# Seven products of quarters for u times w1 in a linear attention and feed-forward kernel

## The chip, the cores and the metric

The kernel runs on one core of a Trainium2 chip. The time is the device time of one execution in microseconds (us), as the median of several runs; the profile is one execution of its own, with a time of its own.

## What is computed

There are 8 batches of 576 rows and 8 heads of 64 columns, so 512 columns in all. The reference, cut to what matters:

```python
kv  = einsum('bhsd,bhse->bhde', k, v)            # per batch and head
out = einsum('bhsd,bhde->bhse', q, kv)
x   = out / sqrt(mean(out * out, -1) + 1e-6) * g_norm
x   = x.transpose(0, 2, 1, 3).reshape(8, 576, 512)
h   = x.transpose(0, 2, 1) @ U @ V               # mixes the rows, rank 32
u   = x + h.transpose(0, 2, 1)
y   = u + maximum(u @ w_ch1, 0) @ w_ch2          # 512 -> 2048 -> 512
```

## The kernel before

All data are float32. To keep the accuracy, the large products are made in three: each factor is split into a high part (rounded to float32r) and a low part (the rest), and high x high, high x low and low x high are added in PSUM.

The rows of u are handled transposed, as four tiles of 128 columns (index c or d) by rows. The 8 x 576 rows are cut into nine **blocks** of 512 (NBLK). Block j needs the end of batch j - 1 and the beginning of batch j. In each block a loop over 16 values of **f** (128 columns of the hidden layer each) makes h for f (`ffn1`, L429: 4 values of d x 3 matmuls of 512 columns, into the one bank of `ps_h`), takes relu and splits it (`relu`, L436: ACT writes the high part hh, DVE the low part hl), and adds the y of the f before (`ffn2`, L445: 4 outputs c x 3 matmuls of 512 columns, into the four banks of `ps_y`). Each matmul has a weight load of its own. In the last block the fourth output is made in two halves of 256 columns, and the last three f's are put together (L757). `finish` (L452) adds u to y, on DVE and POOL, and stores it, after f = 0 of the next block.

All weights stay in SBUF, decoded and split in block 0, in tiles `w_f` with the high and low parts of w1 and w2 for one f (for f = 0 and 1 in tiles of their own).

While block j runs, the kernel **prepares** batch j + 1, in steps placed between the f's by `prep_schedule` (L674) with the distances of `STEPS`. For each of the four pairs of heads p: `kv_step` (L247) makes k times v and loads the next pair; `out_step` (L276) makes q times kv in two PSUM banks; `stats_step`, `mul_step` and `xsplit_step` normalise and split; `turn_step` (L331) transposes in pieces of 32 on DVE and places them by 16 transfers on SP (L343) in `ut32[p]`; then `t_step`, `t4_step` and `mix_step` (L419) multiply by U and V and add (L426) into `ut32[p]`. `split_cols` (L376) writes the factors of the next block, high part on ACT and low part on DVE. The banks for these steps come from `ps_p`, which has three.

All loads and stores are issued by SP. Each engine works its instructions off in a fixed order that a planner of the tile framework sets when the program is built: an instruction earlier in the code goes first, but one that would have to wait can be passed by one that is ready. The start (`ORDER0`) is written out by hand and isn't touched by the change.

Of the kernel before, what the change touches and what calls it, by code (L numbers as in the profile page):

```python
# [10 lines left out]
F32 = mybir.dt.float32  # L11
F32R = mybir.dt.float32r
# [9 lines left out]
P = 128  # L22
# [29 lines left out]
LATE = 8  # L52
LATER = 0
NBLK = B * S // BLK
ABS_LO = float(np.array([897 << 20], np.uint32).view(np.float32)[0])
# [4 lines left out]
def build(ctx: ExitStack, tc: tile.TileContext, kv_in, kvt0_in, kvt_in, q_in, uv_in, g_in, w_in, out):  # L60
# [3 lines left out]
    ldp = ctx.enter_context(tc.tile_pool(name="ldp", bufs=1))  # L64
    utp = ctx.enter_context(tc.tile_pool(name="utp", bufs=2))
    hp = ctx.enter_context(tc.tile_pool(name="hp", bufs=2))
# [8 lines left out]
    x_sb = const.tile([P, NT, P], F32, name="x")  # L75
    ut32 = [const.tile([P, S], F32, name=f"ut32_{c}") for c in range(ND)]
    ident = const.tile([P, P], F32, name="ident")
# [155 lines left out]
    def ut_of(j):  # L233
        if j not in ut:
            ut[j] = [utp.tile([P, ND, BLK], F32R, name=f"ut{s}") for s in "hl"]
        return ut[j]
# [139 lines left out]
    def split_cols(b, c, part, lo_eng):  # L376

        m = BLK * (b + 1) - S * b
        uh, ul = ut_of(b + part)
        if part == 0:  # L380
            src, lo = ut32[c][:, 0:m], BLK - m
        else:
            src, lo = ut32[c][:, m:S], 0
        n = src.shape[-1]
        hi, lo = uh[:, c, lo:lo + n], ul[:, c, lo:lo + n]
        if b == 0:
            split(hi, lo, src, lo_eng)
        else:
            nc.scalar.mul(out=hi, in_=src, mul=g_sb)  # L389
            nc.vector.scalar_tensor_tensor(out=lo, in0=src, scalar=g_sb, in1=hi.bitcast(F32),  # L390
                                           op0=ALU.mult, op1=ALU.subtract)
# [6 lines left out]
    def mix_first(p):  # L398

        s = state[0, p]  # L400
        main = s["main"]
        for a in (0, 2):
            own = main.rearrange("p (i a j) -> p i a j", a=4, j=32)[:, :, a:a + 2]
            v = v4[:, QO[a]:QO[a] + 2 * QL[a]].rearrange("p (a t) -> p a t", a=2)[:, :, 0:P]
            nc.tensor.matmul(own, lhsT=s["t4"], rhs=v.rearrange("p a (i j) -> p i a j", j=32), start=False, stop=(a == 2))
        uh, ul = ut_of(0)
        move("uh", p, uh[:, p], main, g_sb)
        nc.vector.scalar_tensor_tensor(out=ul[:, p], in0=main, scalar=g_sb, in1=uh[:, p].bitcast(F32),
                                       op0=ALU.mult, op1=ALU.subtract)
# [9 lines left out]
    def mix_step(b, p):  # L419
        t4 = state.pop((b, p))["t4"]  # L420
        n = S // 2
        for lo in (0, n):
            mp = bank()[:, 0:n]
            nc.tensor.matmul(mp, lhsT=t4, rhs=v4[:, lo:lo + n], start=True, stop=True)  # L424
            own = ut32[p][:, lo:lo + n]
            nc.vector.tensor_tensor(out=own, in0=mp, in1=own, op=ALU.add)  # L426
        split_cols(b, p, 0, nc.vector)

    def ffn1(h, f, ds, j):  # L429
        uh, ul = ut[j]  # L430
        for d in ds:
            nc.tensor.matmul(h, lhsT=w1s[f][0][:, d, :], rhs=uh[:, d, :], start=(d == 0), stop=False)  # L432
            nc.tensor.matmul(h, lhsT=w1s[f][0][:, d, :], rhs=ul[:, d, :], start=False, stop=False)  # L433
            nc.tensor.matmul(h, lhsT=w1s[f][1][:, d, :], rhs=uh[:, d, :], start=False, stop=(d == ND - 1))  # L434

# [16 lines left out]
    def finish(y, j):  # L452
        uh, ul = ut.pop(j)
        for c, cols, acc in y:
            if j == NBLK - 1:
                o = ut32[c][:, S - BLK + cols.start:S - BLK + cols.stop]
                nc.vector.scalar_tensor_tensor(out=o, in0=o, scalar=g_sb, in1=acc, op0=ALU.mult, op1=ALU.add)
            else:
                o = st.tile([P, DM], F32, name="st")
                nc.vector.tensor_tensor(out=o, in0=acc, in1=uh[:, c, :].bitcast(F32), op=ALU.add)  # L460
                nc.gpsimd.tensor_tensor(out=o, in0=o, in1=ul[:, c, :].bitcast(F32), op=ALU.add)  # L461
            nc.sync.dma_start(out=out[j, c][:, cols], in_=o)

    def outputs(j):

        y = [(c, slice(0, BLK), ps_y.tile([P, BLK], F32, name="y")) for c in range(ND)]
        if j == NBLK - 1:
            c, _, acc = y.pop()
            y.append((c, slice(0, BLK // 2), acc[:, 0:BLK // 2]))
            y.append((c, slice(BLK // 2, BLK), ps_p.tile([P, BLK], F32, name="pp")[:, 0:BLK // 2]))  # L470
        return y

    top = const.tile([P, 2 * DM], U32, name="top")
# [107 lines left out]
    def first_pair(p):  # L581
# [10 lines left out]
        uh, ul = ut_of(0)  # L592
        uh, ul = uh[:, p], ul[:, p]
        xv = x.rearrange("p i (h e) -> p i h e", e=D)
# [79 lines left out]
    def prep_schedule(b):  # L674

        todo = {}
        if 0 < b <= B:
            if b == 1:
                for p in range(NPAIR):
                    todo[REST + 2 * p] = [lambda p=p: mix_rest(p), lambda p=p: split_cols(0, p, 1, nc.vector)]  # L680
            else:
                todo[1] = [lambda: [split_cols(b - 1, c, 1, nc.vector) for c in range(ND)]]
        if b < B:
            for p in range(NPAIR):
                steps = STEPS0 if b == 1 else STEPS
                base = steps["gap"] * p
# [32 lines left out]
    y_prev = hprev = None  # L719
    held = []  # L720
    for j in range(NBLK):
        todo = prep_schedule(j + 1)
        y = None
        for f in range(NF):
            if j == 0:
                while ahead < min(NF, f + 1 + AHEAD):
# [3 lines left out]
                    ahead += 1  # L730
            end = False
            if j == 0 and f == 1:
                ffn2(y, [hprev])
            if j == 0 and f == 0:
                h = h_bank
            else:
                end = j == NBLK - 1 and f == NF - 1
                h = ps_p.tile([P, BLK], F32, name="pp") if end else ps_h.tile([P, BLK], F32, name="h")
                ffn1(h, f, range(ND), j)
            hcur = (f, *relu(h, end))  # L740
            steps = todo.get(2 * f, [])
            for w in steps:
                in_block(j, f, w)
            if hprev is not None and not (j == NBLK - 1 and f > NF - 3) and not (j == 0 and f == 1):
                ffn2(y_prev if f == 0 else y, [hprev])
# [4 lines left out]
            for w in todo.get(2 * f + 1, []):  # L750
                in_block(j, f, w)
            if j == 0 and LATE + f - LATER < NF and f >= LATER:
                load_w(LATE + f - LATER)
            held = (held + [hcur])[-3:]
            hprev = hcur
        y_prev = y
    ffn2(y, held)  # L757
    finish(y, NBLK - 1)


# [54 lines left out]
```

## Time and profile before

| | |
|---|---|
| median of 3 runs | 925.65 us (925.32 to 926.26) |
| the profiled execution | 925.44 us, span 923.7 us |
| TensorE busy | 909.7 us, 4532 matmuls |
| VectorE / ScalarE / GpSimd busy | 402.4 / 271.3 / 47.8 us |
| read from and written to HBM | 46.97 MB and 9.44 MB |
| mean granted TensorE clock | 0.998 |

In the profile, PE is TensorE's matmul, PEld its weight load, DVE VectorE, ACT ScalarE, POOL GpSimd, SP the engine that issues transfers. A group row gives line, engine, operation, what is written and read, the shape and the count; then busy us, the mean ns of one, the idle time of the engine just before them, and what ended it. A row of the waits gives who waited for whom, the us in total, how often, and the longest. A row of the timeline gives start, duration, engine, line, operation and count. Matmuls overlap in the pipeline, so the pace is read from start to start and not from the duration of one.

### The profile page before, as it was taken

To read this page: it belongs to the slowest core of one execution; us is meant where nothing else is said; L and a number is where in the kernel's file an instruction comes from. 1 tells how busy PE (TensorE), PEld (TensorE's weight loads), DVE (VectorE), ACT (ScalarE), POOL (GpSimd) and SP (SyncE) were. 2 spreads that over 40 slices of the span, in tenths; PEclk is the share of its full clock that TensorE was granted. 3 is DMA by queue.
4 is the path that set the end of the run, shared out by engine and by line. 5 is a ranking of instruction groups with operands and counts; after the bars stand their busy time and mean duration, and the time that the engine had idled before them with its cause. 6 is when DMAs were issued, how large, how long until landed. Compare 5 with 4: busy or idle time off the path is not lost.

```text
span 923.7 us, 12114 instructions
## 1 busy us (share of the span) xinstructions
PE 909.7 (98%) x4532; PEld 759.3 (82%) x4532; DVE 402.4 (44%) x870; ACT 271.3 (29%) x572; POOL 47.8 (5%) x61
## 2 busy tenths in 40 slices
PE   8899999999999999999999999999999999999998
PEld 7678888888878888888888888888788888888887
DVE  5789974534344435434344445434334331112112
ACT  5677742322222223222222223222222121111110
POOL 2000002000110002000200010000200020002000
PEclk9999999999999999999999999999999999999999
DMA  9952223211121112212121111212111010001001
GB/s 344 418 202 72 88 68 100 86 32 58 49 81 56 42 62 94 59 32 77 51 60 55 55 65 58 81 32 71 58 49 27 14 46 1 0 1 46 1 1 46
DMA packets 43019, 65.48 MB, mean 71 GB/s; under 512 B 9680, under 2 KB 27856, under 8 KB 42960
## 3 DMA queue, kind: packets, MB, share of 16 engines
q1 hardware_dynamic: 42960, 64.70, 21.0%
q8 instruction: 36, 0.59, 0.3%
q14 instruction: 23, 0.19, 0.1%
HBM read 46.97 MB, written 9.44 MB: 61 GB/s over the span
## 4 chain that ended last, share of the span: by engine, by line
PE 69%; DVE 1%; DMA 0%; POOL 0%; issue 0%; DVEq 0%; POOLq 0%
PE y L449 31%; PE h L432 11%; PE h L433 11%; PE h L434 11%; PE pp L261 2%; PE pp L284 2%; DVE utl L390 1%; PE pp L449 1%; PE pp L354 1%; PE pp L424 0%; PE pp L356 0%; DMA out<-st 0%; DVE st L460 0%; PE pp L286 0%; DVE hl L442 0%; POOL st L461 0%
## 5 line engine op out<-in xcount | busy, mean ns | idle before, releaser
L449 PE MATMUL y<-hh,ws 128*128 128x512 f32 x1000 | 327.9, 394 | 0.0
L442 DVE SCALAR_TENSOR_TENSOR hl<-h,hh 128x512 fp32r<-128x512 f32 x143 | 98.6, 689 | 318.9 <-ACT hh L441 317.7
L449 PEld LDWEIGHTS y<-hh,ws 128*128 128x128 f32 x1000 | 180.9, 188 | 33.1 <-issue 0.2
L441 ACT ACTIVATE hh<-h 128x512 fp32r<-128x512 f32 x143 | 85.4, 597 | 405.4 <-PE h L434 405.4
L432 PE MATMUL h<-uth,ws 128*128 128x512 f32 x500 | 198.0, 396 | 2.1 <-DVE hl L442 2.1
L433 PE MATMUL h<-utl,ws 128*128 128x512 f32 x500 | 195.7, 391 | 0.0
L434 PE MATMUL h<-uth,ws 128*128 128x512 f32 x500 | 195.4, 391 | 0.0
L449 PE MATMUL y<-hl,ws 128*128 128x512 f32 x500 | 193.4, 387 | 0.0
L432 PEld LDWEIGHTS h<-uth,ws 128*128 128x128 f32 x500 | 94.2, 188 | 25.0 <-DVE hl L442 4.3
L434 PEld LDWEIGHTS h<-uth,ws 128*128 128x128 f32 x500 | 94.2, 188 | 20.4
L449 PEld LDWEIGHTS y<-hl,ws 128*128 128x128 f32 x500 | 93.9, 188 | 19.3
L433 PEld LDWEIGHTS h<-utl,ws 128*128 128x128 f32 x500 | 94.4, 189 | 18.5
L461 POOL TENSOR_TENSOR st<-st,utl 128x512 f32<-128x512 f32 x32 | 41.1, 1305 | 782.0 <-DVE st L460 780.6
L449 PE MATMUL y<-hh,w2s 128*128 128x512 f32 (+1 forms) x144 | 47.6, 395 | 2.6 <-ACT hh L441 2.6
L426 DVE TENSOR_TENSOR ut<-pp,ut 128x288 f32<-128x288 f32 x56 | 25.0, 455 | 46.0 <-DMA ut<-xt 30.5
L389 ACT ACTIVATE uth<-ut,g_sb 128x448 fp32r<-128x448 f32 (+7 forms) x56 | 27.6, 531 | 47.7 <-DVE ut L426 25.8
L460 DVE TENSOR_TENSOR st<-y,uth 128x512 f32<-128x512 f32 x32 | 21.4, 686 | 40.3 <-PE y L449 29.1
L449 PEld LDWEIGHTS y<-hh,w2s 128*128 128x128 f32 x144 | 26.5, 188 | 9.4 <-ACT hh L441 4.5
L390 DVE SCALAR_TENSOR_TENSOR utl<-ut,g_sb,uth 128x448 fp32r<-128x448 f32 (+7 forms) x56 | 26.9, 513 | 14.1 <-POOL st L461 6.9
L300 DVE TENSOR_REDUCE sums<-x 128x10 f32<-128x640 f32 x28 | 22.9, 818 | 20.6 <-ACT x L288 20.3
L261 PE MATMUL pp<-kv_sb 128*128 128x128 f32 x224 | 30.3, 274 | 0.0
L284 PE MATMUL pp<-kvb,q_sb 128*128 128x128 f32 x224 | 29.5, 274 | 0.0
(188 smaller groups left out, 852.4 us busy)
## 6 DMA issues: line engine op xcount, KB each, us to landing
kv_sb<-kv_in SPq DMA_DIRECT2D x29, 512.0 KB, 3.5
raw<-w_in SPq DMA_DIRECT2D x14, 1023.6 KB, 15.2
q_sb<-q_in SPq DMA_DIRECT2D x29, 288.0 KB, 2.8
out<-st SPq DMA_DIRECT2D x32, 256.0 KB, 2.0
ut<-xt SPq DMA_DIRECT2D x224, 20.0 KB, 1.8
ut<-xt SPq DMA_DIRECT2D x224, 16.0 KB, 1.8
kvt_sb<-kvt_in SPq DMA_DIRECT2D x27, 128.0 KB, 3.1
kvq<-kv_in SPq DMA_DIRECT2D x3, 512.0 KB, 7.3
```

The costliest lines, as they stand in the source:

```text
L261: nc.tensor.matmul(pp[:, 0:P], lhsT=m[:, i * P:(i + 1) * P], rhs=m[:, MAIN + i * P:MAIN + (i + 1) * P], start=(i == 0 and b < NATIVE), sto ...
L284: nc.tensor.matmul(big[:, i * P:(i + 1) * P], lhsT=qt[:, TAIL + i * P:TAIL + (i + 1) * P], rhs=kb, start=True, stop=True)
L389: nc.scalar.mul(out=hi, in_=src, mul=g_sb)
L390: nc.vector.scalar_tensor_tensor(out=lo, in0=src, scalar=g_sb, in1=hi.bitcast(F32), op0=ALU.mult, op1=ALU.subtract)
L426: nc.vector.tensor_tensor(out=own, in0=mp, in1=own, op=ALU.add)
L432: nc.tensor.matmul(h, lhsT=w1s[f][0][:, d, :], rhs=uh[:, d, :], start=(d == 0), stop=False)
L433: nc.tensor.matmul(h, lhsT=w1s[f][0][:, d, :], rhs=ul[:, d, :], start=False, stop=False)
L434: nc.tensor.matmul(h, lhsT=w1s[f][1][:, d, :], rhs=uh[:, d, :], start=False, stop=(d == ND - 1))
L441: last["relu"] = nc.scalar.activation(out=hh, in_=h, func=AF.Relu)
L442: nc.vector.scalar_tensor_tensor(out=hl, in0=h, scalar=0.0, in1=hh.bitcast(F32), op0=ALU.max, op1=ALU.subtract)
L449: nc.tensor.matmul(acc, lhsT=w2s[f][w][:, c, :], rhs=h[:, cols], start=(f == 0 and w == 0 and h is hh), stop=(f == NF - 1 and w == 1))
L461: nc.gpsimd.tensor_tensor(out=o, in0=o, in1=ul[:, c, :].bitcast(F32), op=ALU.add)
```

## The change

In blocks 0 and 1 the work is as before. From block 2 (FAST) on, u times w1 is made for two f's at a time, a **group** g, in a seven-product form (Strassen's, in Winograd's order of sums). The 512 contracted columns, the 256 columns of w1 and the 512 rows of the block are each halved. Each of the products P1 to P7 contracts 256 (two steps e of 128) for 128 columns of w1 and 256 rows, with three matmuls for high and low parts: 6 matmuls of 256 columns each (`product`).

- **Sums of the weights.** During block 1, after each odd f, `weight_combos` restores w1 of two f's (POOL), makes four sums (DVE), splits them (ACT, DVE) and writes the seven sets by 8 transfers to HBM (`wd`). `make_room` moves w2 of odd f's into the place of w1 of even f's, so that the tiles of odd f's come free.
- **Loads.** From block 2 on, each group's seven sets come back from HBM in two transfers (`load_group`), into two buffers in turn.
- **Factors of u.** The beginnings and ends of batches are brought together in `x32(j)`, by `mix_step` and by `carry` (ACT). `combine` makes the sums of u's quarters and splits them into a ring of ten places: P1, P6 and P5 first (three places that the running block doesn't use), the others one slot later. Both are placed at the last group of the block before.
- **A group.** `fast_group` has two PSUM banks, a (`ps_h`) and b (one of the three of `ps_p`, kept). The pending 24 matmuls of `ffn2` from the group before are dealt out in four quarters (`fill`), with preparing steps behind each. ACT copies partial sums out of the banks, DVE adds them to c22, c21, c12 and c11 in SBUF, and relu and its split follow from there.
- **Finish.** From block 2 on one DVE instruction makes the output from `x32`; POOL's addition goes. In the last block the pending matmuls of the last two f's follow at the end, one f after the other.
- The distances of the preparing steps become `LATER_STEPS`, in quarters of a group, for batches 3 to 7.

```diff
+LATER_STEPS = dict(kv=4, out=5, t=10, mix=10, gap=5)
+COMBINE = 28, 29
+FAST = 2
+NG = NF // 2
+HALF = BLK // 2
+RING = 10
+USE = "P1 P6 P5 P7 P3 P4 P2".split()
...
     def mix_step(b, p):
         t4 = state.pop((b, p))["t4"]
-        n = S // 2
-        for lo in (0, n):
...
+        m = S // 2 if b < FAST else BLK * (b + 1) - S * b
+        for lo, hi in ((0, m), (m, S)):
+            mp = bank()[:, 0:hi - lo]
+            nc.tensor.matmul(mp, lhsT=t4, rhs=v4[:, lo:hi], start=True, stop=True)
+            own = ut32[p][:, lo:hi]
+            to = x32(b)[:, p, BLK - m:] if b >= FAST and lo == 0 else own
+            nc.vector.tensor_tensor(out=to, in0=mp, in1=own, op=ALU.add)
...
+    def carry(j):
+        if j < NBLK - 1:
+            n = S * j - BLK * j
+            nc.scalar.copy(out=x32(j)[:, :, 0:n], in_=ut32_all[:, :, S - n:])
...
+    def combine(j, late):
+        x = x32(j)
+        own = factors.setdefault(j, {name: ring(7 * (j - FAST) + i) for i, name in enumerate(USE)})
+        both = once(("t2", j), lambda: sc.tile([P, 2, HALF], F32, name="t2", tag="xl"))
+        for e in range(2):
+            x11, x12, x21, x22 = [x[:, 2 * k + e, n * HALF:(n + 1) * HALF] for k in range(2) for n in range(2)]
+            t = sc.tile([P, 2, HALF], F32, name="t", tag="xt")
+            t2 = both[:, e]
+            if late:
+                todo = (t[:, 0], x22, x12), (t[:, 1], x21, t2)
+                use = ("P7", t[:, 0]), ("P3", x22), ("P4", t[:, 1]), ("P2", x21)
+            else:
+                todo = (t[:, 0], x12, x11), (t2, x22, t[:, 0])
+                use = ("P1", x11), ("P6", t2), ("P5", t[:, 0])
+            for o, a, b in todo:
+                nc.vector.tensor_tensor(out=o, in0=a, in1=b, op=ALU.subtract)
+            for name, src in use:
+                hi, lo = own[name][:, 0, e], own[name][:, 1, e]
+                nc.scalar.mul(out=hi, in_=src, mul=g_sb)
+                nc.vector.scalar_tensor_tensor(out=lo, in0=src, scalar=g_sb, in1=hi.bitcast(F32),
+                                               op0=ALU.mult, op1=ALU.subtract)
...
+    def weight_combos(i):
+        r = dec.tile([P, 2, DM], F32, name="dec")
+        for k in range(2):
+            nc.gpsimd.tensor_tensor(out=r[:, k], in0=whole(2 * i + k, 0, 0).bitcast(F32), in1=whole(2 * i + k, 0, 1).bitcast(F32),
+                                    op=ALU.add)
...
+        for o, a, b, op in ((s1, a21, a22, ALU.add), (s2, s1, a11, ALU.subtract), (s3, a11, a21, ALU.subtract),
+                            (s4, a12, s2, ALU.subtract)):
+            nc.vector.tensor_tensor(out=o, in0=a, in1=b, op=op)
+        hi = const.tile([P, 4, HALF], F32R, name="sh", tag="top")
+        nc.scalar.copy(out=hi, in_=t)
+        lo = dec.tile([P, 4, HALF], F32R, name="dec")
+        nc.vector.tensor_tensor(out=lo, in0=t, in1=hi.bitcast(F32), op=ALU.subtract)
+        for s, half in enumerate((hi, lo)):
+            nc.sync.dma_start(out=wd[i][:, 1:5, s, :], in_=half.bitcast(F32))
...
+    def make_room(i):
+        if i > 0:
+            to = [whole(2 * i, 0, s) for s in range(2)]
+            for s in range(2):
+                nc.sync.dma_start(out=to[s].bitcast(F32), in_=whole(2 * i + 1, 1, s).bitcast(F32))
+            keep("w2", 2 * i + 1, *to)
...
+    def load_group(k):
+        if k >= NG * (NBLK - FAST) or k in coming:
+            return
+        coming[k] = {}
+        for h, lo, hi in ((0, 0, 4), (1, 4, 7)):
+            n = 2 * (k % 2) + h
+            t = once(("wt", n), lambda: const.tile([P, 4, 2, 2 * P], F32R, name="wt", tag=f"w_{7 + 2 * n}"))
+            nc.sync.dma_start(out=t[:, 0:hi - lo].bitcast(F32), in_=wd[k % NG][:, lo:hi])
...
+    def product(acc, name, j, k, fresh):
+        u, w = factors[j][name], coming[k][name]
+        for e in range(2):
+            for n, (ws_, us) in enumerate(((0, 0), (0, 1), (1, 0))):
+                nc.tensor.matmul(acc, lhsT=w[:, ws_, e * P:(e + 1) * P], rhs=u[:, us, e, :],
+                                 start=fresh and e == 0 and n == 0, stop=e == 1 and n == 2, skip_group_check=not fresh)
...
+    def fast_group(j, g, pending, extra):
+        k = NG * (j - FAST) + g
+        load_group(k)
...
+        product(a, "P1", j, k, True)
+        product(b, "P6", j, k, True)
+        nc.scalar.copy(out=s1, in_=a)
+        nc.scalar.copy(out=s6, in_=b)
+        fill(0)
+        product(a, "P5", j, k, False)
+        product(b, "P7", j, k, False)
+        nc.scalar.copy(out=s15, in_=a)
+        add(c22, b, s15)
+        fill(1)
+        product(a, "P3", j, k, False)
+        product(b, "P4", j, k, False)
+        add(c21, b, s1)
+        add(c12, a, s6)
+        done = [out_of(0)]
+        fill(2)
+        product(b, "P2", j, k, True)
+        add(c11, b, s1)
+        done.append(out_of(1))
+        load_group(k + 1)
+        fill(3)
+        return done
...
             else:
-                todo[1] = [lambda: [split_cols(b - 1, c, 1, nc.vector) for c in range(ND)]]
+                todo[1 if b == FAST else 4] = [lambda: carry(b)]
+                for late in range(2):
+                    todo.setdefault(COMBINE[late], []).append(lambda late=late: combine(b, late))
...
+        if j >= FAST:
+            for g in range(NG):
+                hs = fast_group(j, g, pending, todo)
+                if g == 0:
+                    finish(y_prev, j - 1)
+                    y = outputs(j)
+                pending = []
+                for n, (f, hh, hl) in enumerate(hs):
+                    pending += ffn2_parts(y, f, hh, hl, g == 0 and n == 0, g == NG - 1 and n == 1)
```

More of the change, by code (lines that the diff above doesn't have):

```diff
@@ L234, in ut_of @@
         if j not in ut:
-            ut[j] = [utp.tile([P, ND, BLK], F32R, name=f"ut{s}") for s in "hl"]
+            two = [const.tile([P, 2, 2, BLK], F32R, name="ut", tag=f"u_{2 * j + i}") for i in range(2)]
+            ut[j] = [[t[:, i, s, :] for t in two for i in range(2)] for s in range(2)]
         return ut[j]
@@ L420, in mix_step @@
         t4 = state.pop((b, p))["t4"]
-        n = S // 2
-        for lo in (0, n):
[L423 to L427, printed above, removed]
+        m = S // 2 if b < FAST else BLK * (b + 1) - S * b
[5 more added lines that the diff above has]
+            nc.vector.tensor_tensor(out=to, in0=mp, in1=own, op=ALU.add)
+        if b < FAST:
+            split_cols(b, p, 0, nc.vector)
     def ffn1(h, f, ds, j):
@@ L471, in outputs, with once, x32 @@
         return y
+    kept = {}
+    def once(key, make):
+        if key not in kept:
+            kept[key] = make()
+        return kept[key]
+    def x32(j):
+        if j == NBLK - 1:
+            return ut32_all[:, :, S - BLK:]
+        return once(("x32", j % 2), lambda: const.tile([P, ND, BLK], F32, name="x32", tag=f"u_{2 * (j % 2)}"))
+    def carry(j):
+        if j < NBLK - 1:
+            n = S * j - BLK * j
+            nc.scalar.copy(out=x32(j)[:, :, 0:n], in_=ut32_all[:, :, S - n:])
@@ new lines, in ring, with slot @@
+    def ring(i):
+        def slot(tag, n):
+            t = once(("ring", tag), lambda: const.tile([P, n, 2, 2, HALF], F32R, name="uc", tag=tag))
+            return [t[:, k] for k in range(n)]
+        i %= RING
+        if i < 4:
+            return slot(f"w_{3 + 2 * (i // 2)}", 2)[i % 2]
+        if i < 6:
+            return slot(f"w1_{i - 4}", 1)[0]
+        return slot(f"u_{1 + 2 * ((i - 6) // 2)}", 2)[i % 2]
+    factors = {}
+    def combine(j, late):
[19 more added lines that the diff above has]
+                                               op0=ALU.mult, op1=ALU.subtract)
@@ new lines, in ffn2_parts, with part, fill, out_of @@
+    def ffn2_parts(y, f, hh, hl, first, last):
+        def part(c, cols, acc, w, h, start, stop):
+            return lambda: nc.tensor.matmul(acc, lhsT=w2s[f][w][:, c, :], rhs=h[:, cols], start=start, stop=stop)
+        return [part(c, cols, acc, w, h, first and n == 0, last and n == 2) for c, cols, acc in y
+                for n, (w, h) in enumerate(((0, hh), (0, hl), (1, hh)))]
+    def fast_group(j, g, pending, extra):
+        k = NG * (j - FAST) + g
+        load_group(k)
+        a = once("a", lambda: ps_h.tile([P, BLK], F32, name="h"))[:, 0:HALF]
+        b = once("b", lambda: ps_p.tile([P, BLK], F32, name="pp"))[:, 0:HALF]
+        t = once(("t", k % 2), lambda: dec.tile([P, 4, HALF], F32, name="dec"))
+        s1, s6, s15 = [t[:, i] for i in range(3)]
+        sums = once("sums", lambda: const.tile([P, 2, BLK], F32, name="sums2", tag="top"))
+        c11, c12, c21, c22 = [sums[:, i, n * HALF:(n + 1) * HALF] for i in range(2) for n in range(2)]
+        q = (len(pending) + 3) // 4
+        add = lambda o, x, y: nc.vector.tensor_tensor(out=o, in0=x, in1=y, op=ALU.add)
+        def fill(n):
+            for what in pending[n * q:(n + 1) * q]:
+                what()
+            for what in extra.get(4 * g + n, []):
+                what()
+        def out_of(i):
+            hh, hl = h_unit((2 * k + i) % 4)
+            nc.scalar.activation(out=hh, in_=sums[:, 1 - i], func=AF.Relu)
+            nc.vector.scalar_tensor_tensor(out=hl, in0=sums[:, 1 - i], scalar=0.0, in1=hh.bitcast(F32),
+                                           op0=ALU.max, op1=ALU.subtract)
+            return 2 * g + 1 - i, hh, hl
+        product(a, "P1", j, k, True)
[20 more added lines that the diff above has]
+        return done
@@ L730, in build @@
                     ahead += 1
-            end = False
             if j == 0 and f == 1:
@@ L751, in build @@
                 in_block(j, f, w)
+            if j == 1 and f % 2 == 0 and f > 0:
+                make_room(f // 2 - 1)
             if j == 0 and LATE + f - LATER < NF and f >= LATER:
                 load_w(LATE + f - LATER)
-            held = (held + [hcur])[-3:]
             hprev = hcur
+        if j == 1:
+            pending = ffn2_parts(y, *hprev, False, True)
+            pending[-1] = (lambda last=pending[-1]: (last(), make_room(NG - 1)))
         y_prev = y
-    ffn2(y, held)
+    for what in pending:
+        what()
     finish(y, NBLK - 1)
```

68 lines of the change are left out of this document (46 added, 22 removed).

## The prediction

> **What bounds the kernel now.** I read the page's first lines, then TensorE's waits, then the chain of work, then the timeline at TensorE alone.
>
> ```profile
> span 923.7 us, 12114 instructions
> PE 909.7 (98%) x4532; PEld 759.3 (82%) x4532; DVE 402.4 (44%) x870; ACT 271.3 (29%) x572; POOL 47.8 (5%) x61
> ```
> ```profile
> PE y L449 <- ACT hh L441: 2.6, 3, 1.6
> ```
>
> TensorE is busy 98% of the span, and the longest entry of its waits comes to 2.6 us in all. Nothing else limits this kernel: a change pays only by what it takes off TensorE's stream, and costs whatever makes TensorE wait. A busy share isn't a rate, so I take the rate from start to start. Here is the chain in a block with little beside the two products, then the last block, whose fourth output is made in halves of 256 columns, and the end of the program.
>
> ```profile
> 735.26 2.72 PE y L449 x12
> ...
> 740.70 2.72 PE y L449 x12
> ```
> ```profile
> 903.09 0.28 PE L449 MATMUL y<-hl,ws 128*128 128x256 f32 x1
> ...
> 903.56 0.98 PE L449 MATMUL y<-hh,ws 128*128 128x512 f32 x4
> 904.38 0.28 PE L449 MATMUL pp<-hh,ws 128*128 128x256 f32 x1
> 904.50 0.40 PE L432 MATMUL h<-uth,ws 128*128 128x512 f32 x1
> ```
> ```profile
> 918.89 0.28 PE L449 MATMUL y<-hl,ws 128*128 128x256 f32 x1
> ...
> 919.96 0.28 PE L449 MATMUL pp<-hh_end,ws 128*128 128x256 f32 x1
> 920.28 0.48 DVE L457 SCALAR_TENSOR_TENSOR ut<-ut,g_sb,pp 128x256 f32<-128x256 f32 x1
> ```
>
> One f (12 matmuls for h, 12 for y) takes 740.70 - 735.26 = 5.44 us, so a 512-column matmul with its own weights costs 5.44 / 24 = 0.2267 us. From 918.89 to 919.96 lie ten matmuls of 256 columns, nine steps: 1.07 / 9 = 0.1189 us each. That is 52% of the price of the wide one, again with a weight load for each. The change lives on this number. The other two readings bound it: 903.09 to 903.56 holds four in 0.47 us (0.1175), and 903.09 to 904.50 holds six of 256 and three of 512: (1.41 - 3 x 0.2267) / 6 = 0.1217, with the switches between widths put on the narrow ones.
>
> **What leaves and enters TensorE's stream.** For two f's, u times w1 now takes 24 wide matmuls: 24 x 0.2267 = 5.44 us. In the seven-product form a product is 2 (halves of the contraction) x 3 (high and low parts) = 6 matmuls of 256 columns, and seven are 42: 42 x 0.1189 = 4.99 us. It saves 0.45 us a group, and there are 8 groups in each of the blocks 2 to 8: 56 x 0.446 = 25.0 us. By the bounds it is 56 x (5.44 - 4.935) = 28 us and 56 x (5.44 - 5.111) = 18 us. I take 25, since the run of ten is the nearest to the product's run of 12. The saving ends where a narrow matmul costs 5.44 / 42 = 0.1295 us: only 9% above what is seen.
>
> In the Trainium skill, "TensorE: Matmul & The Clock Gate", section "Back-to-back issue gap", a rule speaks against the change: in a stream of weight loads and matmuls both set the pace, and it gives 81 ns a matmul at 128 columns and 131 ns at 512. My estimate from that page by a straight line is 98 ns at 256 columns, so a group would go from 24 x 131 to 42 x 98 ns, 1.0 us more. This trace doesn't agree: 226.7 ns at 512 columns and 118.9 at 256 nearly halve.
>
> **What the other engines get, and what hides it.**
>
> ```profile
> L434 PEld LDWEIGHTS h<-uth,ws 128*128 128x128 f32 x500 | 94.2, 188 | 20.4
> L442 DVE SCALAR_TENSOR_TENSOR hl<-h,hh 128x512 fp32r<-128x512 f32 x143 | 98.6, 689 | 318.9 <-ACT hh L441 317.7
> L441 ACT ACTIVATE hh<-h 128x512 fp32r<-128x512 f32 x143 | 85.4, 597 | 405.4 <-PE h L434 405.4
> L256 ACT CAST tails<-kvt_sb 128x256 fp32r<-128x256 f32 x24 | 9.6, 401 | 14.1 <-PE pp L259 13.5 <-DMA kvt_sb<-kvt_in 0.5
> L426 DVE TENSOR_TENSOR ut<-pp,ut 128x288 f32<-128x288 f32 x56 | 25.0, 455 | 46.0 <-DMA ut<-xt 30.5 <-PE pp L424 8.6 <-PE h L434 5.9
> L390 DVE SCALAR_TENSOR_TENSOR utl<-ut,g_sb,uth 128x256 fp32r<-128x256 f32 x8 | 3.5, 475 | 1.2 <-ACT uth L389 1.2
> L225 DVE TENSOR_TENSOR ws<-dec,ws 128x1024 fp32r<-128x1024 f32 x14 | 17.0, 1216 | 1.7 <-ACT ws L221 1.7
> L461 POOL TENSOR_TENSOR st<-st,utl 128x512 f32<-128x512 f32 x32 | 41.1, 1305 | 782.0 <-DVE st L460 780.6
> ```
>
> A group: TensorE spends 4.99 + 24 x 0.2267 = 10.4 us. ACT gets three copies of 256 columns (0.40 each) and two relus (0.60): 2.4 us. DVE gets four sums (at most 0.455, the 288-column row) and two low halves (0.69): 3.2 us. The order inside the group decides. A quarter of the pending y matmuls is 6 x 0.2267 = 1.36 us, and two products are 1.43. From the group's start: P1 and P6 to 1.43, fill to 2.79, P5 and P7 to 4.22, fill to 5.58, P3 to 6.29, P4 to 7.0, fill to 8.36, P2 to 9.1, fill to 10.4. Bank b, read by the sum c22 at about 4.3 to 4.8, is overwritten by P4 at 6.29: 1.5 us to spare. c21 reads it from 7.1 to 7.6, P2 overwrites it at 8.36: 0.8 us. c11 from 9.2 to 9.7 against the next P6 at 11.1: 1.4 us. Each of these spares is longer than one DVE instruction of the table but the longest, so another step's work ahead in DVE's queue costs at times, not always. What waits behind a late sum is everything on TensorE's queue. I price it at 0.05 us a group, 56 x 0.05 = 3 us; bounds are 0 (as now, where 98% is busy) and 0.3 us, 17 us in all (half the smallest spare lost to an instruction of 0.69 in every group).
>
> Factors of u: the splits of L389 and L390 go from all later blocks, and a block gets 14 narrow splits and 8 subtractions: 22 x 0.475 = 10.5 us on DVE, 14 between 0.40 and 0.60 on ACT, some 7 us. The first set (P1, P6, P5) goes to three free places of the ring of ten; the others may follow while group 7 and the next group 0 run. Only the first set is on a path, and it is priced with the chain below. The mix matmuls keep their 576 columns, cut elsewhere, and the output's addition on POOL goes from the later blocks; neither was waited for, so 0.
>
> Block 1 also makes the weight sums: per group 2 x 1.3 us on POOL, four sums (under 0.5) and one low half of 1.2 on DVE, a copy of 1024 columns on ACT (twice 0.6), all beside about 11 us of TensorE. Cover is there; each instruction is short against the two f's. SP gets 8 transfers a group and 14 moves, 78 in block 1.
>
> ```profile
> 452.93 4.57 SPq L462 DMA_DIRECT2D out<-st  x4
> 457.75 7.48 SPq L343 DMA_DIRECT2D ut<-xt  x12
> ...
> 468.07 10.76 SPq L343 DMA_DIRECT2D ut<-xt  x16
> 478.93 0.53 SPq L169 DMA_DIRECT2D kv_sb<-kv_in  x1
> ...
> 493.29 10.93 SPq L343 DMA_DIRECT2D ut<-xt  x16
> ...
> 512.02 10.00 SPq L343 DMA_DIRECT2D ut<-xt  x16
> ...
> 551.60 4.57 SPq L462 DMA_DIRECT2D out<-st  x4
> ```
>
> SP takes 0.53 us to issue a large load and 10.76 / 16 = 0.67 for a turned piece, so 78 more take 41 to 52 us of a block of 551.60 - 452.93 = 98.7 us, in which SP issues four runs of about 10 us already. It fits, with little over. Batch 2's turned pieces slip behind them; if all that SP has is delayed, the first products of block 2 wait. I put 3 us, once, for this and for the first weights; bounds 0 and 10 (a run of turned pieces).
>
> The end: the last 24 y matmuls go unit by unit rather than output by output, so DVE's last additions queue: an output comes every 3 x 0.2267 = 0.68 us while DVE needs 0.69 for 512 columns (L442, the same width and kind) and twice 0.48 (the row at 920.28) for the halves, the last of which come 0.36 apart. That is at most two such additions: 0.8 us.
>
> **The transfers of the weights.** Landing times of now, and two stretches, whose last two columns are the DMA engines' share and GB/s:
>
> ```profile
> kv_sb<-kv_in SPq DMA_DIRECT2D x29, 512.0 KB, 3.5
> raw<-w_in SPq DMA_DIRECT2D x14, 1023.6 KB, 15.2
> ...
> ut<-xt SPq DMA_DIRECT2D x224, 20.0 KB, 1.8
> ```
> ```profile
> 0.00:30.00 30.00, 25.18 (x175) 22.38 (x175) 17.43 (x53) 18.01 (x48) 6.68 (x29) 1.00 0.95 360
> 430.00:530.00 100.00, 100.00 (x498) 83.55 (x498) 41.75 (x95) 25.66 (x60) 5.08 (x4) 1.00 0.19 58
> ```
>
> A group loads 7 x 2 x 256 words for 128 partitions: 1.84 MB. At the 360 GB/s of the first 30 us that is 5.1 us, and there are about 12 (98.7 / 8). The buffers are double and free once the group before last is over, so I cost it at nothing: it is covered by one group of TensorE. The engines' share goes from 0.19 to some 0.6, and a piece of 20 KB behind such a load lands up to 5 us later, part of the chain's price below. The load's issue waits in SP's queue for the last product of the group before last; behind it stand the turned pieces and the k, v and q loads, and mix waits for those. That too could lengthen a cycle of the chain, never by more than a group.
>
> **The chain that prepares the next batch.** This is the one thing with little cover left. Per pair of heads: out (two PSUM banks), normalise, turn, 16 transfers on SP, mix, which needs the landed pieces, and its sums free banks for the next out. The SP lines show the beat: runs start at 457.75, 468.07, 493.29 and 512.02, so a cycle was 10.3 (its out had run ahead), 25.2 and 18.7 us. The long one has a load of k and v behind the run, at 478.93. From the stores to the end of the fourth run is 522.0 - 452.9 = 69.1 us.
>
> After the change, bank b keeps one of three, so the second pair's out can't run ahead: all three cycles are full ones. The next block's first product must find its factors. Counted from the stores, it is due at 98.7 - 8 x 0.446 - 10.4 = 84.7 us (its own stores follow its group 0, 10.4 us, where they now follow the first f, 5.44). The chain ends at 4.8 (first run) + three cycles + 10 (fourth run) + 2.3 (landing 1.8 and a sum) + 4.8 (ten DVE instructions of the first set). With cycles of 18.7 it is 78; with 22 (the mean of the two full ones) 88; with 25.2, 97.5. The point where it meets 84.7 is a cycle of 20.9 us. If later than due, TensorE waits at the end of blocks 2 to 6, five times. I take 1 us each, 5 us: nearer the cycle of 18.7, since the load behind the run, which made one cycle long, was absent from the other.
>
> **Sum**, against the profiled execution (925.44 us, 1.7 of it outside the span; 0.2 under the median of 925.65, which I leave aside): -25 + 3 (inside groups) + 3 (block 1 and start of 2) + 0.8 (end) + 5 (chain) = -13.2, so 912.2: **912 us**.
>
> **Rivals.**
> *The preparing chain becomes the bound (slower).* Place: ends of blocks 2 to 6; it decides from a cycle of 20.9 us on. At 25.2, seen once, TensorE waits 12.8 us five times: 912 - 5 + 64 = 971. At 22, 3.2 x 5 = 16: 923. In between, at 23, it is 6.2 x 5 = 31: 938, the price I give it. For it: two banks, heavier SP and DMA queues, a DVE with (41.75 - 16 x 0.69 - 8 x 0.475 + 8 x 3.2 + 10.5) / 96 = 66% rather than 42% to do. Against: SP's runs end early now, and the spare was 551.6 - 5.4 - 522.0 = 24 us. Chance 0.20.
> *A narrow matmul runs at the weight load's pace.* The row of L434 shows 188 ns for one load; if the loads of a longer narrow run didn't overlap, 56 x (42 x 0.188 - 5.44) = +138 in place of -25: 912 + 163 = 1075. The run of ten at 0.1189 speaks against it. Chance 0.03. The Trainium skill's rule named above is this mechanism in a milder size.
> *The weight loads aren't hidden.* At the kv load's speed, 1.84 MB takes 3.6 x 3.5 = 12.6 us against about 12: 0.6 x 56 = 34: 946. The 15.2 us of the raw loads were under a full start, so they bound it from above (two of them, 27 us, would double the time). Chance 0.05.
> *All of it is covered:* only -25 + 0.8: 901. Chance 0.12.
> The forecast itself: 0.60, with its own range of 904 to 922.
>
> **The numbers.** 0.2%, about what this measurement can tell, is 1.9 us. Faster: the forecast 0.59, all covered 0.12, low end of the chain 0.02: 0.73. Same: 0.05, the chain at a cycle near 22 and the forecast's top. Slower: 0.22, the rest. The range goes from 899 (the gain of 28 us less little) to 940 (the chain at 23 us); outside are some 0.06 below and 0.14 above.
>
> **What would show it.** Matmuls of 128x256 from start to start at 0.119 us inside products, and 56 x 66 of both widths: right on the main term. TensorE's waits: entries of a or b on ACT's copies and DVE's sums, near 3 us in all; first products on the low halves of the factors, near 5 us. SP's runs of turned pieces 19 to 21 us apart: right; 23 or more with TensorE idle at block ends: the first rival. Products waiting on the weight tiles: the third. Wrong altogether if narrow matmuls stand over 0.1295 us apart.

## The result, and the profile after

The kernel with the seven products takes 934.05 us (median of 4 runs, 931.56 to 934.92), the kernel before in the same series 925.78 us (925.32 to 926.26, 4 runs). The ratio is 1.0085 (95% interval 1.0063 to 1.0107): 0.85% slower, where 912 us was forecast. The profiled execution took 934.86 us with a span of 933.1 us, 9.4 us over the span of before.

The page's first lines and the longest of TensorE's waits (who waited for whom, us in total, times, longest) are now:

```profile
span 933.1 us, 15120 instructions
PE 899.6 (96%) x5540; PEld 794.5 (85%) x5540; DVE 548.1 (59%) x1236; ACT 362.5 (39%) x800; POOL 37.7 (4%) x53
```
```profile
PE h L443 <- DVE hl L453: 5.9, 5, 2.4
PE pp L597 <- DVE sums L626: 5.0, 10, 1.2
PE y L460 <- ACT hh L452: 2.3, 2, 1.6
PE h L597 <- ACT dec L648: 2.1, 4, 0.6
...
PE h L597 <- ACT dec L643: 1.4, 3, 0.5
...
PE h L597 <- DMA wt<-wd: 0.9, 1, 0.9
```

TensorE was busy 909.7 us and is busy 899.6: the work did shrink. New in the waits are the products (L597) behind DVE's sums (L626) and ACT's copies (L643, L648), 8.5 us by these three rows. That is not yet the loss, for this view counts only gaps in which TensorE is seen idle, and matmuls overlap in the pipeline. So I add up, over the trace, the time from each matmul's start to the next one's start, by what the matmul belongs to (a wait then stands with the matmul ahead of it):

| us | before | after | difference |
|---|---|---|---|
| u times w1 in blocks 2 to 8 | 308.5 (1344 of 512 columns) | 307.2 (2352 of 256) | -1.3 |
| u times w1 in blocks 0 and 1 | 93.9 | 93.9 | 0 |
| y | 405.4 | 407.6 | +2.2 |
| preparing | 111.1 | 117.0 | +5.9 |
| from the last matmul's start to the end | 3.7 | 6.3 | +2.6 |

Before the first matmul lies about 1 us in both. At the forecast's 0.1189 us, 2352 narrow matmuls are 279.6 us: 28.9 us less than what they replace. Only 1.3 us of it came. The products hold 27.6 us that the price of a matmul doesn't explain, 0.49 us in each of 56 groups; their mean step is 130.6 ns, though the median is the forecast's, between 119 and 120 ns. Something stands between the matmuls, and the timeline of TensorE in block 7, which prepares no batch, shows what:

```profile
789.13 0.88 PE L597 MATMUL pp<-uc,wt 128*128 128x256 f32 x6
789.85 0.88 PE L597 MATMUL h<-uc,wt 128*128 128x256 f32 x6
790.56 0.94 PE L597 MATMUL pp<-uc,wt 128*128 128x256 f32 x6
791.34 0.89 PE L597 MATMUL h<-uc,wt 128*128 128x256 f32 x6
792.06 0.94 PE L597 MATMUL pp<-uc,wt 128*128 128x256 f32 x6
792.84 1.10 PE L610 MATMUL y<-h_more,ws 128*128 128x512 f32 x4
793.77 0.88 PE L597 MATMUL h<-uc,wt 128*128 128x256 f32 x6
794.49 2.00 PE L610 MATMUL y<-h_more,ws 128*128 128x512 f32 x8
796.33 0.88 PE L597 MATMUL pp<-uc,wt 128*128 128x256 f32 x6
```

This is not the order of the code. Bank a (`h`) runs part of a group ahead of bank b (`pp`): from 789.13 stand P7, P1 of the next group, P4, P5 of the next group and P2, five products back to back, and only then four matmuls of y; then P3 of the next group, eight of y, and P6. In the code a quarter of the pending y matmuls, six, lies between each two pairs. Here is what must happen to a bank between two of its products:

```profile
790.04 0.42 DVE L626 TENSOR_TENSOR sums<-pp,dec 128x256 f32<-128x256 f32 x1 [2.58 <-PE pp L597]
790.82 0.37 ACT L643 COPY dec<-h 128x256 f32<-128x256 f32 x1 [3.81 <-PE h L597]
791.54 0.43 DVE L626 TENSOR_TENSOR sums<-pp,dec 128x256 f32<-128x256 f32 x1 [1.07 <-PE pp L597]
```

P7 ends at 790.01 (789.13 + 0.88). DVE reads its bank from 790.04 to 790.46, and P4, which overwrites it, starts at 790.56 and takes 0.78 us to the next product's start (791.34), where an undisturbed one takes 0.72 (789.13 to 789.85). P2 stands in the same way behind the sum at 791.54 and takes 0.78. With one product of 0.72 us as the only cover, even an idle DVE is late by a hair. Over the whole trace the 27.6 us are made up so: 148 times a product's first step, to its second matmul, is longer by 76 ns in the mean (45 of them in the 56 P4 and 45 in the 56 P2), 11.2 us together; 19 times a product starts between 0.16 and 1.03 us late behind another, 10.3 us; 4.6 us lie between a product and other work behind it, and 1.5 us are scattered. Of the 19, ten are two products in a row on the same bank, with no cover at all (6.7 us); eight times DVE or ACT had other work ahead (2.6 us), and once a weight load was late (1.0 us). Not all of the 27.6 us belongs to the two banks: 3.3 of the 4.6 us are preparing steps that wait for their own bank or input, and about 1.1 us comes from a stretch of 3.4 us, right behind the longest of these waits, in which the granted clock was 0.5 and a narrow matmul took 213 ns.

### The profile page after: what moved, and what is told of

It is laid out like the page before. It is cut to its first block, busy times and chain, and to the rows that moved or that the text cites. A ratio compares the mean times of both kernels' runs of the same rounds, so it can differ in the third digit from the quotient of the medians.

```text
span 933.1 us, 15120 instructions
## 1 busy us (share of the span) xinstructions
PE 899.6 (96%) x5540; PEld 794.5 (85%) x5540; DVE 548.1 (59%) x1236; ACT 362.5 (39%) x800; POOL 37.7 (4%) x53
## 4 chain that ended last, share of the span: by engine, by line
PE 76%; DMA 8%; DVE 8%; SPq 3%; ACT 2%; issue 2%; POOL 0%; DVEq 0%; ACTq 0%; POOLq 0%
PE y L610 30%; PE pp L597 16%; PE h L597 11%; PE y L460 4%; DMA wt<-wd 3%; SPq L352 3%; PE pp L270 2%; PE pp L293 2%; PE h L443 2%; PE h L444 2%; PE h L445 2%; DMA out<-st 1%; DMA wd<-dec 1%; DMA ut<-xt 1%; DMA kvq<-kv_in 1%
## 5 line engine op out<-in xcount | busy, mean ns | idle before, releaser
L597 PE MATMUL pp<-uc,wt 128*128 128x256 f32 x1344 | 206.2, 289 | 5.3 <-DVE sums L626 5.0
L597 PEld LDWEIGHTS pp<-uc,wt 128*128 128x128 f32 x1344 | 180.3, 190 | 14.4 <-DVE sums L626 8.0
L610 PE MATMUL y<-h_more,ws 128*128 128x512 f32 (+1 forms) x672 | 168.2, 391 | 0.2 <-DVE h_more L637 0.2
L597 PE MATMUL h<-uc,wt 128*128 128x256 f32 x1008 | 150.4, 285 | 4.4 <-ACT dec L648 2.1
L597 PEld LDWEIGHTS h<-uc,wt 128*128 128x128 f32 x1008 | 134.7, 191 | 10.4 <-ACT dec L648 2.9
L610 PEld LDWEIGHTS y<-h_more,ws 128*128 128x128 f32 x672 | 120.7, 189 | 21.5 <-DVE h_more L637 0.3
L626 DVE TENSOR_TENSOR sums<-pp,dec 128x256 f32<-128x256 f32 x168 | 70.7, 421 | 100.8 <-PE pp L597 98.9
L610 PE MATMUL y<-hh,ws 128*128 128x512 f32 x344 | 112.8, 391 | 0.0
L460 PE MATMUL y<-hh,ws 128*128 128x512 f32 x216 | 71.9, 398 | 0.0
L610 PEld LDWEIGHTS y<-hh,ws 128*128 128x128 f32 x344 | 62.1, 189 | 10.6 <-ACT hh L636 0.4
L643 ACT COPY dec<-h 128x256 f32<-128x256 f32 x56 | 20.7, 369 | 123.8 <-PE h L597 121.8
L626 DVE TENSOR_TENSOR sums<-h,dec 128x256 f32<-128x256 f32 x56 | 23.7, 424 | 71.2 <-ACT dec L644 68.5
L443 PE MATMUL h<-ut,ws 128*128 128x512 f32 x112 | 45.2, 403 | 5.9 <-DVE hl L453 5.9
L637 DVE SCALAR_TENSOR_TENSOR h_more<-sums,h_more 128x512 fp32r<-128x512 f32 x56 | 38.5, 687 | 20.9 <-ACT h_more L636 20.8
L460 PEld LDWEIGHTS y<-hh,ws 128*128 128x128 f32 x216 | 38.8, 188 | 7.6 <-issue 0.3
L444 PE MATMUL h<-ut,ws 128*128 128x512 f32 x112 | 43.8, 391 | 0.0
L445 PE MATMUL h<-ut,ws 128*128 128x512 f32 x112 | 43.8, 391 | 0.0
```

Of the source, the lines that this page charges most:

```text
L443: nc.tensor.matmul(h, lhsT=w1s[f][0][:, d, :], rhs=uh[d], start=(d == 0), stop=False)
L444: nc.tensor.matmul(h, lhsT=w1s[f][0][:, d, :], rhs=ul[d], start=False, stop=False)
L445: nc.tensor.matmul(h, lhsT=w1s[f][1][:, d, :], rhs=uh[d], start=False, stop=(d == ND - 1))
L460: nc.tensor.matmul(acc, lhsT=w2s[f][w][:, c, :], rhs=h[:, cols], start=(f == 0 and w == 0 and h is hh), stop=(f == NF - 1 and w == 1))
L597: nc.tensor.matmul(acc, lhsT=w[:, ws_, e * P:(e + 1) * P], rhs=u[:, us, e, :], start=fresh and e == 0 and n == 0, stop=e == 1 and n == 2, ...
L610: return lambda: nc.tensor.matmul(acc, lhsT=w2s[f][w][:, c, :], rhs=h[:, cols], start=start, stop=stop)
```

## The experiments

Theory A: the 27.6 us are waits for the two banks to be read out, since five products stand back to back with nothing between. Rivals: B, that narrow matmuls over two widths cost more than 0.119 us by themselves; C, that the weight loads (1.84 MB a group) slow TensorE or what feeds it. The first four kernels ran together, beside a kernel before of 924.44 us.

**The products without the wait for the read-out.** ACT and DVE do as much as before, on a tile in SBUF that never changes.

```diff
+        still = uf.rearrange("p i r -> p (i r)")[:, 0:HALF]
-        nc.scalar.copy(out=s1, in_=a)
-        nc.scalar.copy(out=s6, in_=b)
+        nc.scalar.copy(out=s1, in_=still)
+        nc.scalar.copy(out=s6, in_=still)
...
-        add(c11, b, s1)
+        add(c11, still, s1)
```

> The changed kernel, but the copies and sums that follow the products read a fixed tile in SBUF and no longer the two PSUM banks; what is left out is that the products reach h. All matmuls, copies, sums, relus and transfers remain in number and size. Theory A (the products wait for the two banks to be read out, 24 to 27 us in all, because they stand together with no y matmuls between): about 911 us, between 905 and 917. Theory B (256-column matmuls in the new stream cost some 0.131 us by themselves): no change, 931 to 937. Theory C (the weight reloads slow the stream): no change either.

Measured: 909.83 us, ratio 0.9841 (0.9827 to 0.9856). The page's first line, and the two groups of products (busy us, mean ns of one, idle before); in the changed kernel they have 289 and 285 ns, and 5.3 and 4.4 us of idle time:

```profile
span 907.6 us, 14930 instructions
```
```profile
L597 PE MATMUL pp<-uc,wt 128*128 128x256 f32 x1344 | 197.7, 284 | 0.0
...
L597 PE MATMUL h<-uc,wt 128*128 128x256 f32 x1008 | 152.6, 284 | 0.3 <-DMA wt<-wd 0.3
```

From start to start the products now take 284.8 us (121.1 ns each): 22.4 of the 27.6 us are gone with nothing taken off TensorE, and of the 148 late first steps 24 are left. Theory A has its first support. It isn't alone decisive: freed of the banks, the planner also mixes the products otherwise, and some 4 of the 22.4 us are the preparing steps' waits and the low clock, which this run's products don't have.

**Narrow matmuls without the seven products.** The kernel before, from block 2 on with u times w1 in halves of 256 columns: twice the matmuls, the same banks and order.

```diff
+        if j >= 2:
+            for cols in (slice(0, 256), slice(256, 512)):
+                for d in ds:
+                    for n, (w, u) in enumerate(((0, uh), (0, ul), (1, uh))):
+                        nc.tensor.matmul(h[:, cols], lhsT=w1s[f][w][:, d, :], rhs=u[:, d, cols], ...)
```

> The kernel before, with one change: from block 2 on each 512-column matmul of u times w1 is made as two of 256 columns. No sums, no bank reuse, no reload: only 1344 wide matmuls become 2688 narrow ones. Theory A: they cost 0.119 us each, 2688 x 0.119 - 1344 x 0.2267 = +15 us, 941. Theory B: 0.1306 us each, +46 us, 972. Theory C says nothing of it (as A).

Measured: 944.01 us, ratio 1.0211 (1.0196 to 1.0227). The timeline, where from the first row to the third lie 24 narrow matmuls, and then 12 of y (the rows between are left out):

```profile
784.45 0.28 PE L435 MATMUL h<-uth,ws 128*128 128x256 f32 x1
784.56 0.28 PE L435 MATMUL h<-utl,ws 128*128 128x256 f32 x1
...
787.32 0.40 PE L456 MATMUL y<-hl,ws 128*128 128x512 f32 x1
...
790.07 0.28 PE L435 MATMUL h<-uth,ws 128*128 128x256 f32 x1
```

(787.32 - 784.45) / 24 = 0.1196 us for a narrow one and (790.07 - 787.32) / 12 = 0.2292 for a wide one. Over all 2688 the mean from start to start is 120.2 ns, so the price on which the forecast lived holds, and theory B falls. The time is 3 us over theory A's 941; y alone takes 409.5 us where it took 405.4, in matmuls of the same number and width. By the Trainium skill, "TensorE: Matmul & The Clock Gate", section "Back-to-back issue gap", with its 81 ns at 128 columns and 131 at 512, a straight line (an estimate) would put a narrow one at three quarters of a wide one; here it is 52%, so the measurement decides against that page for these matmuls.

**The written order, held.** As the changed kernel, but each quarter of y is queued behind the products ahead of it in the code, and the next products behind that quarter. No wait is taken away; only TensorE's order is fixed.

```diff
+        def queued(acc, names, fresh):
+            with (tc.issue_after(behind[0].ins) if behind[0] is not None else ExitStack()):
+                for bank, name in zip(acc, names):
+                    ahead_of[0] = product(bank, name, j, k, fresh)
...
-            for what in pending[n * q:(n + 1) * q]:
-                what()
+            with tc.issue_after(ahead_of[0].ins):
+                for what in pending[n * q:(n + 1) * q]:
+                    got = what()
+                    behind[0] = got[0] if isinstance(got, tuple) else got
...
-        product(a, "P1", j, k, True)
-        product(b, "P6", j, k, True)
+        queued((a, b), ("P1", "P6"), True)
```

> The changed kernel with the written order held on TensorE's queue: each fill of y matmuls is queued behind the products before it, and the next products behind that fill. Nothing else differs. Theory A: by the times of one group every read-out of a bank is covered by a fill, so most of the 24 us of waits in the products go; 911 to 921 us, below the kernel before. Theory B: 934, no change. Theory C: 934, no change. If the held order makes TensorE wait for hl or for the preparing steps instead, it is above 934.

Measured: 915.57 us, ratio 0.9906 (0.9891 to 0.9921). The intervals lie apart: by the two ratios this is 1.8% (17 us) below the changed kernel, for an order alone. TensorE's timeline:

```profile
774.48 0.88 PE L597 MATMUL h<-uc,wt 128*128 128x256 f32 x6
775.20 0.88 PE L597 MATMUL pp<-uc,wt 128*128 128x256 f32 x6
775.91 1.55 PE L611 MATMUL y<-h_more,ws 128*128 128x512 f32 x6
777.30 0.88 PE L597 MATMUL h<-uc,wt 128*128 128x256 f32 x6
778.01 0.88 PE L597 MATMUL pp<-uc,wt 128*128 128x256 f32 x6
778.74 1.55 PE L611 MATMUL y<-h_more,ws 128*128 128x512 f32 x6
```

Two products, six of y, two products: between P1 at 774.48 and P5 at 777.30, which takes the same bank, now lie 2.82 us. The products take 289.7 us (123.2 ns each), with 77 late first steps and one pair on the same bank. Of the 17.5 us that are gone, some 4 are again the preparing steps' waits and the low clock. Together with the first kernel this shows theory A for most of the 27.6 us: fixed order or absent read-out, either brings back most of the gain, at the same count and size of matmuls. Of the 10 us that are left over 279.6, 3.2 stand in group 0 of the blocks, where finishing comes in, and 1.6 in group 1; the rest is spread over the other six, and what causes it was not taken apart.

**No reload of the weights.** Only the first two groups' weights are loaded.

```diff
-            nc.sync.dma_start(out=t[:, 0:hi - lo].bitcast(F32), in_=wd[k % NG][:, lo:hi])
+            if k < 2:
+                nc.sync.dma_start(out=t[:, 0:hi - lo].bitcast(F32), in_=wd[k % NG][:, lo:hi])
```

> The changed kernel, but only the first two groups' weights are loaded from HBM and all later groups use them again; what is left out is the reload of the right weights (54 of 56 groups, some 99 MB). Theory A: the reload is covered, 931 to 935 us (the few us of weight waits and late turned pieces go). Theory B: 931 to 935. Theory C: the reload costs the missing time, under 920 us.

Measured: 926.72 us, ratio 1.0017 (1.0005 to 1.0029), between the two expectations. Against the changed kernel the ratios differ by 0.68%, some 6 us (the spans by 7.6): theory C is right in a small part. The products still take 301.0 us, so it isn't what ate the gain.

Four more kernels ran together, beside a kernel before of 925.36 us. **The same on the written order**, that is, the third kernel without reloads:

> The held order of e3 and, as in e4, only the first two groups' weights loaded (what is left out is the reload of the right weights). Theory A: the 7 us that the reload cost in the bunched order were small delays with no cover; with fills between the products they are covered: 913 to 916, at most 3 us below e3. Theory C in its small form (the reload costs some 7 us whatever the order): 907 to 910.

Measured: 911.77 us, ratio 0.9863 (0.9849 to 0.9876), 0.43% or 4.0 us below the third kernel's ratio, again between. So the loads cost some 4 us in the written order as well; whether that is less than the 6 us of the planner's order can't be told, since each difference of two ratios is uncertain by about 0.2%, some 2 us. Where the 4 us arise isn't settled: products, y and the end each give up about a microsecond.

**Block 1: the weights restored on DVE, not on POOL.** The trace of the changed kernel shows in block 1 three stalls of TensorE, 1.23, 1.41 and 2.58 us (from start to start, over an undisturbed step). Around the longest, the engines POOL and DVE, then TensorE:

```profile
188.23 2.53 POOL L551 TENSOR_TENSOR dec<-ws 128x512 f32<-128x512 f32 x2 [16.40 <-DVE r L312]
188.33 1.22 DVE L313 TENSOR_TENSOR ta<-r,half 128x10 f32<-128x10 f32 x1
189.58 1.20 DVE L314 TENSOR_TENSOR ta<-ta,r 128x10 f32<-128x10 f32 x1
190.82 0.17 DVE L315 SCALAR_TENSOR_TENSOR half<-ta,r 128x10 f32<-128x10 f32 x1
...
191.83 0.67 DVE L453 SCALAR_TENSOR_TENSOR hl<-h,hh 128x512 fp32r<-128x512 f32 x1
...
192.56 0.50 PE L443 MATMUL h<-ut,ws 128*128 128x512 f32 x1 [2.42 <-DVE hl L453]
```

Two DVE instructions on ten columns take 1.22 and 1.20 us while POOL's two sums run (188.23 to 190.76); the third of that size takes 0.17 as soon as POOL is done. The low half of h, which frees the bank, stands behind them in DVE's queue.

```diff
-            nc.gpsimd.tensor_tensor(out=r[:, k], in0=whole(2 * i + k, 0, 0).bitcast(F32), ...)
+            nc.vector.tensor_tensor(out=r[:, k], in0=whole(2 * i + k, 0, 0).bitcast(F32), ...)
```

> The changed kernel with one edit in block 1: w1 is restored (high plus low part, 16 sums of 512 columns) on DVE in place of POOL. Theory A with its block 1 part (two small DVE instructions of 0.17 us took 1.2 us each while POOL added, and TensorE waited 5.2 us for hl in block 1): DVE takes 16 x 0.69 = 11 us more in block 1, where it has room, and the three waits of 1.2 to 2.6 us go: 929 to 933 us. Rival: the waits come from DVE's amount of work in block 1; then 11 us more on it makes them longer, 935 to 940.

Measured: 931.35 us, ratio 1.0067 (1.0055 to 1.0080). By time alone this can't be told from the changed kernel. The trace tells: the first product of block 2 starts at 230.6 us in place of 234.8, and the waits have

```profile
PE h L443 <- DVE hl L453: 2.7, 3, 1.5
```

in place of 5.9. Moving the sums is worth some 4 us by the start of block 2, but they don't explain all three stalls. At the one of 1.23, DVE's low half of the weight sums (L562) took 2.11 us, where it takes 1.22 otherwise, beside POOL's addition for an output (L470), which stays. At the one of 1.41 no DVE instruction is stretched: the low half of h stands behind such a low half (1.21 us) and a transpose (0.83). And with the sums on DVE one stall of 1.70 us is left, with POOL idle, behind DVE's own work. So the rival holds for a part.

**The last outputs in place.** In the changed kernel the last five outputs share three buffers. Its end on DVE:

```profile
925.76 2.06 DVE L472 SCALAR_TENSOR_TENSOR st<-ut,g_sb,y 128x512 f32<-128x512 f32 x3 [2.01 <-PE y L610]
928.68 0.48 DVE L472 SCALAR_TENSOR_TENSOR st<-ut,g_sb,y 128x256 f32<-128x256 f32 x1 [0.86 <-DMA out<-st]
929.37 0.48 DVE L472 SCALAR_TENSOR_TENSOR st<-ut,g_sb,pp 128x256 f32<-128x256 f32 x1 [0.21 <-DMA out<-st]
```

The fourth addition waits 0.86 us for the store of the first, the fifth 0.21. Before, the last block was written in place.

```diff
+                own = x32(j)[:, c, cols]
+                o = own if j == NBLK - 1 else o
-                nc.vector.scalar_tensor_tensor(out=o, in0=x32(j)[:, c, cols], scalar=g_sb, in1=acc, ...)
+                nc.vector.scalar_tensor_tensor(out=o, in0=own, scalar=g_sb, in1=acc, ...)
```

> The changed kernel, but the last block's five outputs are written where x32 lies, as in the kernel before, and not into the three buffers for stores. The two waits on DMA out<-st after the last matmul (0.86 and 0.21 us, and what queued behind) should go: the tail from the last matmul's start, 6.3 us, falls towards the 3.7 of before: 931 to 933 us. Rival: DVE's queue of five additions sets the tail, not the buffers; then it stays at 934.

Measured: 931.42 us, ratio 1.0073 (1.0061 to 1.0086); again not to be told from the changed kernel by time. From the last matmul's start to the end it takes 5.4 us, not 6.3; the expected fall to that of before (3.7) didn't come, since DVE's five additions still stand one behind the other, until 1.8 us after the last matmul's start (0.8 before).

**All three:** written order, weights restored on DVE, last outputs in place.

> The held order of e3, the sums of block 1 on DVE and the outputs in place, together. Theory A: the three are in different places and add up: 915.6 less 2 to 5 less 1 to 3, 908 to 912 us, 1.4 to 1.8% below the kernel before. Rival: what is saved in block 1 returns as a wait at the start of block 2, where the first factors are late; then 913 to 915.

Measured: 910.70 us (910.17 to 911.37), ratio 0.9847 (0.9833 to 0.9860): 1.5% below the kernel before and, by the two ratios, 2.4% below the kernel as changed. It is the version to keep. TensorE is busy 888.6 us of a span of 909.0, and products take 290.2 us from start to start.

## Why the prediction was wrong, step by step

The forecast has a span of 910.5 us, the trace 933.1; the 22.6 us between them fall out as follows.

| step of the prediction | forecast | measured | difference |
|---|---|---|---|
| 1344 wide ones against 2352 narrow at 0.1189 | -25.0 | -28.9 | -3.9 |
| waits inside groups | 3 | 27.6 | +24.6 |
| block 1 and start of block 2 | 3 | 5.2 | +2.2 |
| preparing chain and all else in y and preparing | 5 | 2.9 | -2.1 |
| end | 0.8 | 2.6 | +1.8 |

- **The main term** was right. The narrow price stands (0.1196 in the halves, the products' median at 0.119 to 0.120); the wide ones that left had cost 3.9 us more than 1344 x 0.2267, with their small waits.
- **"Inside groups", 0.05 us a group, is the step that failed.** It read the spare of bank b (1.5, 0.8 and 1.4 us) from the order of the statements, and of bank a, where 31 of the 148 late steps and six of the ten pairs stand, it read none. The planner lets an instruction that is ready pass one that would wait, as the description of the kernel says, and the y matmuls, the only cover, were not where the code has them. With five products in a row the cover of a read-out is one product, 0.72 us, and the spare is nothing. 0.49 us a group lies outside the step's own bound of 0.3 too, and so do the 20.5 us of late steps, pairs and late readers alone (0.37). What the step did price, another step's work ahead in an engine's queue, came to 2.6 us, near its 3. With the order that the step had assumed, held by force, the products lose 10.1 us in place of 27.6; with block 1 and the end mended too, the time is 910.7 us. That this is near the 912 forecast is in part luck: the products still lose 10.6 us there where 3 had been put, while the wide matmuls that left had cost more than forecast.
- **Block 1**: of the forecast's reason (SP delayed, turned pieces late) the trace shows nothing; the size came near by other causes, which "cover is there" had passed by: DVE held while POOL added, and DVE's own queue. That is luck. The three stalls are 5.2 us, and the DVE version took 4.2 off the start of block 2.
- **The chain** came near its price: 2.9 us, or 6.2 with the 3.3 us of preparing steps that the sum over the products holds. The largest piece, 1.9 us, is the step of q times kv in block 5, waiting for a bank that an addition of the mix step frees. SP's runs of turned pieces in block 4:

```profile
461.04 8.49 SPq L352 DMA_DIRECT2D ut<-xt  x12
478.04 10.53 SPq L352 DMA_DIRECT2D ut<-xt  x16
500.26 10.90 SPq L352 DMA_DIRECT2D ut<-xt  x16
524.07 10.58 SPq L352 DMA_DIRECT2D ut<-xt  x16
```

  They stand 17.0, 22.2 and 23.8 us apart, a mean of 21.0, where the rival decided from 20.9 on; the last run ends at 534.65 and the first product of block 5 starts at 544.0, with no wait for a factor of u. So a mean of 21.0 did not yet bind. The rival on the slower side did not come, so the sign was wrong for a reason that no rival named.
- **Reload of weights**, priced at 0 for being covered: 4 us in the written order, some 6 in the planner's. TensorE waited for a weight tile itself only 0.9 us. The median landing times are now these; the turned pieces take 0.3 us more than before:

```profile
wt<-wd SPq DMA_DIRECT2D x56, 1024.0 KB, 5.3
wt<-wd SPq DMA_DIRECT2D x56, 768.0 KB, 5.5
...
ut<-xt SPq DMA_DIRECT2D x224, 20.0 KB, 2.1
```

- **The end**: DVE's queue was named; the buffers of the stores (0.86 + 0.21 us) were overlooked. Without them 5.4 of the 6.3 us stay, 1.7 more than before.

## What to carry to other kernels

Where a planner orders an engine's queue, the spare between the reader of a bank and its next writer has to be read from the order it makes, or the order has to be held; the order of the statements proves nothing. A change to shorter matmuls also shortens the cover of every read-out beside them, so price the read-out (end of one product to the release of its bank) against what stands between, before counting the gain. And where such a change brings nothing, fix the order before dropping it: here the order alone takes the same arithmetic from 0.85% slower to 0.94% faster, and two smaller edits bring it to 1.5%.

## What the runs showed of the hardware that was not expected

- DVE instructions with two operands in SBUF stand still while POOL adds. In the changed kernel, those of L313 and L314 on ten columns take 169 ns in the mean with no addition of POOL beside them (53 of them) and 0.62, 1.20 and 1.22 us with one (3); those of L453, which read one operand from PSUM, take 679 ns in the mean without (25) and 680 with one (7). The Trainium skill, "SBUF — State Buffer", section "Who interferes with whom", says that a DVE instruction with two SBUF operands and a GpSimd one that reads SBUF shut each other out for a whole instruction, and that one with a single SBUF operand, outside DVE's two-port modes, goes free. The trace agrees in both: one of POOL's two sums takes about 1.27 us (2.53 for both).
- A wait that ends just in time isn't free for narrow matmuls: 76 ns on a step of 119, in 148 products, while TensorE's own waits list hardly any of them. The mean from start to start (130.6 ns) shows what the idle columns don't. The weight loads show where it enters: P4's first load starts at 790.52, 0.05 us behind the end of DVE's sum and 78 ns behind the start of the matmul ahead, where the loads before it follow within 2 ns; it ends at 790.71, and P4's second matmul starts at 790.75. In the 148 products the first load starts 33 ns ahead of its matmul in the mean, in the other 244 it starts 164 ns ahead.
